# Joined row statistics for the two heads of a pair in the first batch of an attention and two-FFN kernel

## The chip, the cores and the metric

The kernel runs on one core of a Trainium2 chip. The time is the device time of one execution in microseconds (us), and lower is better. The engines are called as in the profile: PE (TensorE: matmuls and transposes; PEld are its weight loads), DVE (VectorE), ACT (ScalarE), POOL (GpSimd) and SP (SyncE, which issues most of the transfers). Each engine works through its own list in order and waits on semaphores of the others.

## The reference

Causal attention with a decay bias, then two feed-forward layers (FFNs), all in float32:

```python
def _attn_ref(q, k, v, s):          # 4 batches, 8 heads, 576 positions, 64 columns
    scores = q @ k.T / sqrt(D)
    cum = np.cumsum(np.maximum(s, 0.0), axis=-1)
    bias = -(cum[:, :, :, None] - cum[:, :, None, :])
    scores = np.where(causal, -1e9, scores + np.minimum(bias, 0.0))
    scores = scores - np.max(scores, axis=-1, keepdims=True)
    attn = np.exp(scores)
    attn = attn / (np.sum(attn, axis=-1, keepdims=True) + 1e-09)
    return attn @ v
# FFN 1: h = x @ w_in (512 -> 1024), softmax-gated, normalised, @ w_out (1024 -> 512), 2304 tokens
# FFN 2: h = x @ w2_in (512 -> 2048), h * clip(h + 3, 0, 6) / 6, @ w2_out (2048 -> 512)
```

The change lies in the attention: the maximum of each row of scores, and the reciprocal of each row's sum.

## The kernel before

The work is staged in three plans. The first holds all of the attention, the decoding of FFN 1's weights and most of FFN 1; the others hold the rest of FFN 1 and FFN 2. In a plan, each piece of work is added with its engine, a cost, and the names of what it reads and writes; `Plan.emit` then walks through time with these costs and writes out one list for each engine, always taking the earliest added piece that is ready. So the order on every engine follows from all the costs and dependencies together, and one piece more or less can move many others. Scores and FFN products share eight PSUM banks (`bank`), which the plan hands out too.

Attention goes by heads. A head's 576 rows are cut into five tiles t = 0 to 4 of 128, 128, 128, 96 and 96 rows; tile t needs the columns up to its own end, so tile 4 has 576 columns, too many for one bank, and comes in two pieces of 288. In batch 0 the two heads of a pair are worked on together (`qk_whole`, four pairs); later batches take one head at a time (`qk`). For each piece PE makes the scores (L545 in batch 0, L572 later), and `tops` on DVE (L501) adds the mask, copies the piece to SBUF (`y`) and puts the negated row maximum into `nmax`. For tile 4 the maxima of the two pieces are joined by `both` (L509). ACT then takes the exponential in place (L513) and puts the row sums into `sums`. When a head's five tiles are done, `norm` makes the reciprocals on DVE (L583, L584 into `rsum`), and POOL multiplies the five tiles by them (L588). PE transposes the blocks (L634), DVE and ACT copy them out (L638), PE multiplies them with V (L663), and DVE and ACT copy the result into `x` (L670). In batch 0's pairs 1 and 3 the score tiles lie in the buffers named zhy and zly. The last pair of batch 0 is normalised by `norm_part`, which already takes both heads in a call (L601, L602, L606).

Between these the plan puts the decoding of the weights, which come as 64-bit numbers: a load issued by ACT (raw_wi, L301), a step on ACT (L307), three on DVE (L311, L316, L319), one on POOL (L323), the high part (L329 or L331) and the low part on POOL (L337). Queries and keys are loaded by SP (rawq, rawk, L383), and values too (V, L395 and L396). From pair 4 on (batch 1) they are turned on PE (L451), split into high and low parts (HL4q and the like, L459 and L463; pair 4's keys use the free end of w_out_l), and copied by SP into two operand buffers stack0 and stack1, one for each head of a pair (L469, L470); the gate rows, rows_d, are loaded into them last (L473). The first L572 of a head needs all of these. FFN 1 follows: L740 for h, L751 to L781 for its statistics, L806 to L813 for the transposed parts zh and zl, and L827 for its output.

## Time and profile before

| what | value |
|---|---|
| median of 3 timed runs | 854.26 us (854.06 to 858.12) |
| span of the profiled execution | 851.3 us, so the median lies 2.96 us above it |
| PE, DVE, ACT, POOL busy | 813.4, 484.0, 399.2, 226.6 us |
| batch 0's pieces of L509, and of L583 with L584 before the joined pair 3 | 8, and 6 of each |

Busy time is that of the engine's own instructions. The span runs from the first to the last instruction; the timed runs have a small part around it. Batch 0 and the turn to batch 1 lie in the first 100 us or so.

### The profile page before, as it was taken

Reading aid. Unit: us, or ns where it says so; the run is one execution under the profiler, and the core shown is the slowest. Engines: PE = TensorE matmul, PEld = TensorE weight load, DVE = VectorE, ACT = ScalarE, POOL = GpSimd, SP = SyncE. Lnnn points to the kernel's source line nnn. Section 1 sums busy time; section 2 is a strip of 40 time slices with the busy share of each in tenths; the row PEclk is TensorE's granted clock in tenths of the full one; section 3 lists DMA queues with packets and bytes.
Section 4 is the critical chain, followed back from the end, with each engine's and each line's share of the span. In section 5 each row is a group of like instructions: output and inputs, shape, how many; then the busy total and the mean of one; then the engine's idle time right before and its main releaser. Section 6 shows DMA issues by size and latency. Waiting matters only on the chain.

```text
span 851.3 us, 13524 instructions
## 1 busy us (share of the span) xinstructions
PE 813.4 (96%) x4816; PEld 686.6 (81%) x4816; DVE 484.0 (57%) x1205; ACT 399.2 (47%) x928; POOL 226.6 (27%) x323
## 2 busy tenths in 40 slices
PE   3997899999999999999999999999999999999998
PEld 2565677888898889887798999998888888888886
DVE  4898999556755575648746999843222232222221
ACT  2776767646665465635444555444222322232222
POOL 1686666334533263325320112100000000000000
PEclk9999999999999999999999999999999999999999
DMA  6569476655555455233304444112000300010001
GB/s 167 129 156 204 124 172 135 151 125 114 128 137 126 98 115 125 63 111 108 104 32 162 143 129 137 63 62 87 0 1 2 99 0 1 1 49 1 1 1 50
DMA packets 93667, 76.85 MB, mean 90 GB/s; under 512 B 62080, under 2 KB 75904, under 8 KB 93600
## 3 DMA queue, kind: packets, MB, share of 16 engines
q1 hardware_dynamic: 91296, 67.60, 31.4%
q10 hardware_dynamic: 2304, 8.39, 3.1%
q8 instruction: 38, 0.62, 0.3%
q14 instruction: 29, 0.24, 0.1%
HBM read 44.71 MB, written 10.03 MB: 64 GB/s over the span
## 4 chain that ended last, share of the span: by engine, by line
PE 79%; DVE 11%; DMA 4%; POOL 3%; issue 1%; ACT 1%; SPq 0%; ACTq 0%; DVEq 0%; POOLq 0%
PE bank L986 23%; PE bank L1017 23%; PE bank L827 11%; PE bank L740 8%; PE bank L663 4%; PE bank L572 4%; PE bank L634 4%; PE bank L806 1%; DVE y L501 1%; PE bank L451 1%; POOL y L588 1%; DMA rawk<-in_k_dram 1%; DVE st L751 1%; DMA stack<-rows_d 1%; PE bank L545 1%
## 5 line engine op out<-in xcount | busy, mean ns | idle before, releaser
L986 PE MATMUL bank<-x2h,w 128*128 128x512 f32 (+1 forms) x640 | 185.4, 371 | 0.0
L1017 PE MATMUL bank<-w,gh 128*128 128x512 f32 x576 | 178.5, 393 | 0.6 <-ACT gh L998 0.6
L994 DVE SCALAR_TENSOR_TENSOR g<-g,bank 128x512 f32<-128x512 f32 (+1 forms) x80 | 50.5, 632 | 184.1 <-ACT g L990 183.9
L986 PEld LDWEIGHTS bank<-x2h,w 128*128 128x128 f32 x640 | 118.6, 188 | 18.7
L990 ACT ACTIVATE g<-bank 128x512 f32<-128x512 f32 (+1 forms) x80 | 44.4, 555 | 176.4 <-PE bank L986 176.1
L1017 PEld LDWEIGHTS bank<-w,gh 128*128 128x128 f32 x576 | 107.8, 188 | 23.2 <-ACT gh L998 1.2
L986 PE MATMUL bank<-x2l,w 128*128 128x512 f32 (+1 forms) x320 | 118.5, 370 | 0.0
L1017 PE MATMUL bank<-w,gl 128*128 128x512 f32 x288 | 111.4, 391 | 0.0
L588 POOL TENSOR_SCALAR y<-y,rsum 128x128 f32<-128x128 f32 (+4 forms) x140 | 80.7, 593 | 99.7 <-DVE rsum L584 55.4
L501 DVE CUSTOM_DVE_ANT_0 y<-bank,mask 96x288 f32<-96x288 f32 (+4 forms) x168 | 74.1, 466 | 48.0 <-PE bank L572 38.8
L513 ACT ACTIVATE y<-y,nmax 128x256 f32<-128x256 f32 (+4 forms) x140 | 83.5, 597 | 32.9 <-DVE nmax L501 26.8
L827 PE MATMUL bank<-zh,w_out_h 128*128 128x256 f32 x288 | 83.2, 289 | 0.3 <-DVE nmax L501 0.3
L827 PE MATMUL bank<-zl,w_out_h 128*128 128x256 f32 x288 | 81.2, 282 | 1.9 <-DVE zl L813 1.9
L827 PE MATMUL bank<-zh,w_out_l 128*128 128x256 f32 x288 | 81.0, 281 | 0.0
L1002 DVE TENSOR_TENSOR gl<-g,gh 128x512 fp32r<-128x512 f32 (+1 forms) x80 | 56.2, 703 | 36.2 <-ACT gh L998 35.5
L998 ACT CAST gh<-g 128x512 fp32r<-128x512 f32 (+1 forms) x80 | 46.1, 577 | 46.2 <-DVE g L994 45.7
L986 PEld LDWEIGHTS bank<-x2l,w 128*128 128x128 f32 x320 | 60.0, 188 | 8.2
L1017 PEld LDWEIGHTS bank<-w,gl 128*128 128x128 f32 x288 | 54.1, 188 | 11.9
L572 PE MATMUL bank<-stack 128*96 128x288 f32 (+4 forms) x288 | 58.9, 318 | 4.9 <-DMA stack<-rows_d 2.3
L740 PE MATMUL bank<-w_in_h,xh 128*128 128x512 f32 x144 | 61.5, 427 | 1.1 <-DVE xh L722 0.6
L740 PE MATMUL bank<-w_in_h,xl 128*128 128x512 f32 x144 | 58.0, 403 | 1.0 <-POOL xl L726 1.0
L740 PE MATMUL bank<-w_in_l,xh 128*128 128x512 f32 x144 | 57.7, 401 | 0.0
(170 smaller groups left out, 1388.6 us busy)
## 6 DMA issues: line engine op xcount, KB each, us to landing
raw_w2i<-in_moe_w_in_dram SPq DMA_DIRECT2D x16, 512.0 KB
raw_w2o<-in_moe_w_out_dram SPq DMA_DIRECT2D x16, 512.0 KB
rawq<-in_q_dram SPq DMA_DIRECT2D x32, 144.0 KB
rawk<-in_k_dram SPq DMA_DIRECT2D x32, 144.0 KB
x_d<-x2s SPq DMA_DIRECT2D x36, 128.0 KB
out_dram<-ob SPq DMA_DIRECT2D x18, 256.0 KB
raw_wi<-in_moe_w_in_dram ACTq DMA_DIRECT2D x8, 512.0 KB
raw_wo<-in_moe_w_out_dram ACTq DMA_DIRECT2D x8, 512.0 KB
```

Of the source, the lines that this page charges most:

```text
L501: nc.vector.tensor_tensor_reduce(out=ys[h, t][:n, c0:c1], in0=bank(key)[:n, : c1 - c0], in1=mask[:n, 480 + n - w + c0 : 480 + n - w + c1], ...
L513: nc.scalar.activation(out=y[:n], in_=y[:n], func=AF.Exp, bias=nmax[:n, h, t : t + 1], scale=-1.0, accum_out=sums[:n, h, t : t + 1])
L572: nc.tensor.matmul(bank(key)[:n, : c1 - c0], lhsT=ss[:, 2 - 2 * m, ST[t] : w], rhs=ss[:, 3 - 2 * m, c0:c1], start=(m == 0), stop=(m == 1))
L588: nc.gpsimd.tensor_scalar(ys[h, t][:n], ys[h, t][:n], rsum[:n, h, t : t + 1], 1.0, ALU.mult, ALU.mult)
L740: nc.tensor.matmul(bank(key), lhsT=xs[i][m // 2][:, kk, :], rhs=(w_in_l if m == 1 else w_in_h)[:, kk, f * 512 : (f + 1) * 512], start=(kk ...
L827: nc.tensor.matmul(bank(key)[:, : 2 * P], lhsT=w[:, kk, m * P : (m + 1) * P], rhs=z[:, kk, :], start=(kk == 0 and i == 0), stop=(kk == KFF ...
L986: nc.tensor.matmul(bank(key)[:, :w], lhsT=wt[:, a, 0, c * P : (c + 1) * P], rhs=x[:, c, :w], start=(c == 0 and i == 0), stop=(c == KDM - 1 ...
L990: nc.scalar.activation(out=g_t[ci, m][0][:, :w], in_=bank(key)[:, :w], func=AF.Relu, bias=3.0, scale=1.0)
L994: nc.vector.scalar_tensor_tensor(out=gg, in0=gg, scalar=6.0, in1=bank(key)[:, :w], op0=ALU.min, op1=ALU.mult)
L998: nc.scalar.copy(gh[:, :w], gg[:, :w])
L1002: nc.vector.tensor_sub(gl[:, :w], gg[:, :w], gh[:, :w].bitcast(F32))
L1017: nc.tensor.matmul(bank(key), lhsT=g_t[ci, m][1 + i // 2][:, t * P : (t + 1) * P], rhs=w2[m][:, i % 2, 1, :], start=(m == 0 and i == 0), s ...
```

## The change

For batch 0 the join of the two pieces' maxima, and the reciprocals of the row sums, are done in one call for both heads of a pair. In `pieces`, `norm` now gets the list of heads, which has one head in the later batches. The multiplications on POOL are added in the order tile by tile, head by head within a tile, where before one head's five came first. The line numbers shift: L509 becomes L510, L513 L514, L572 L573, L583 and L584 L586 and L587, L588 L591, L634 and L638 L638 and L642, L663 L667, L740 L744, L827 L831.

```diff
-    def exps(h, t, pieces):
+    def exps(heads, t, pieces):
         n, w = SZ[t], ST[t] + SZ[t]
+        hs = slice(heads[0], heads[-1] + 1)
 
         def both():
-            nc.vector.tensor_tensor(nmax[:n, h, t : t + 1], nmax[:n, h, t : t + 1], nmax[:n, h, NQ : NQ + 1], ALU.min)
-
-        def exp():
+            nc.vector.tensor_tensor(nmax[:n, hs, t : t + 1], nmax[:n, hs, t : t + 1], nmax[:n, hs, NQ : NQ + 1], ALU.min)
+
+        def exp(h):
             y = ys[h, t]
...
         if len(pieces) > 1:
-            plan.add("DVE", 0.2, both, reads=[f"nmax{h}_{NQ}"], writes=[f"nmax{h}_{t}"])
+            plan.add("DVE", 0.2, both, reads=[f"nmax{h}_{NQ}" for h in heads], writes=[f"nmax{h}_{t}" for h in heads])
...
-    def norm(h):
+    def norm(heads):
+        hs = slice(heads[0], heads[-1] + 1)
+
         def inv():
-            nc.vector.tensor_scalar_add(rsum[:, h, :], sums[:, h, :], 1.0e-9)
-            nc.vector.reciprocal(rsum[:, h, :], rsum[:, h, :])
+            nc.vector.tensor_scalar_add(rsum[:, hs, :], sums[:, hs, :], 1.0e-9)
+            nc.vector.reciprocal(rsum[:, hs, :], rsum[:, hs, :])
...
-        plan.add("DVE", 0.34, inv, reads=[f"sums{h}_{t}" for t in range(NQ)], writes=[f"rsum{h}"])
+        plan.add("DVE", 0.36, inv, reads=[f"sums{h}_{t}" for h in heads for t in range(NQ)], writes=[f"rsum{h}" for h in heads])
         for t in range(NQ):
-            plan.add("POOL", 0.27 + 0.00085 * (ST[t] + SZ[t]), lambda t=t: go(t), reads=[f"rsum{h}", f"{y_key(h, t)}/e"], writes=[f"{y_key(h, t)}/n"])
+            for h in heads:
+                plan.add("POOL", 0.27 + 0.00085 * (ST[t] + SZ[t]), lambda h=h, t=t: go(h, t), reads=[f"rsum{h}", f"{y_key(h, t)}/e"], writes=[f"{y_key(h, t)}/n"])
...
-            elif x == "n":
-                r.extend((0.0, lambda h=h: norm(h)) for h in last)
+            elif x == "n" and last:
+                r.append((0.0, lambda: norm(last)))
```

On DVE, the list at the reciprocals of pair 0 (e_wi and a_wi are the second block of w_in in decoding, HL the queries and keys of pair 2):

```order
 L501 ISA nmax 128x1
-L583 TENSOR_SCALAR rsum<-sums 128x5
-L584 RECIPROCAL rsum<-rsum 128x5
-L316 TENSOR_SCALAR e_wi_0_326<-a_wi_0_300 128x512
-L583 TENSOR_SCALAR rsum<-sums 128x5
-L584 RECIPROCAL rsum<-rsum 128x5
-L319 SCALAR_TENSOR_TENSOR e_wi_0_326<-raw_wi_0_159,e_wi_0_326 128x512
+L316 TENSOR_SCALAR e_wi_0_319<-a_wi_0_300 128x512
+L319 SCALAR_TENSOR_TENSOR e_wi_0_319<-raw_wi_0_159,e_wi_0_319 128x512
+L586 TENSOR_SCALAR rsum<-sums 128x10
+L587 RECIPROCAL rsum<-rsum 128x10
 L420 COPY HL_265<-bank_102 128x288
```

Four calls became two, and they moved behind the two decode steps. On POOL, the multiplications of pair 0 (y_0 to y_4 are tiles, a_wi and w_in_l as above); before:

```order
L337 TENSOR_TENSOR w_in_l<-a_wi_0_173,w_in_h 128x512
L588 TENSOR_SCALAR y_0_175<-y_0_175,rsum 128x128
L588 TENSOR_SCALAR y_1_191<-y_1_191,rsum 128x256
L588 TENSOR_SCALAR y_2_212<-y_2_212,rsum 128x384
L588 TENSOR_SCALAR y_3_224<-y_3_224,rsum 96x480
L588 TENSOR_SCALAR y_4_238<-y_4_238,rsum 96x576
L588 TENSOR_SCALAR y_0_176<-y_0_176,rsum 128x128
```

and now:

```order
L337 TENSOR_TENSOR w_in_l<-a_wi_0_173,w_in_h 128x512
L323 TENSOR_TENSOR a_wi_0_300<-a_wi_0_300,e_wi_0_319 128x512
L591 TENSOR_SCALAR y_0_175<-y_0_175,rsum 128x128
L591 TENSOR_SCALAR y_0_176<-y_0_176,rsum 128x128
L591 TENSOR_SCALAR y_1_191<-y_1_191,rsum 128x256
L591 TENSOR_SCALAR y_1_192<-y_1_192,rsum 128x256
L591 TENSOR_SCALAR y_2_212<-y_2_212,rsum 128x384
```

The heads alternate, and the decode step L323 moved ahead of all ten. On SP's queue, the loads at the turn to batch 1 (numbers behind the names are pairs, for stack the head of the pair); before:

```order
L383 DMA rawk5_664<-in_k_dram 96x6x64 x2
L395 DMA V3_631<-in_v_dram 128x3x64
L396 DMA V3_631<-in_v_dram 96x2x64
L469 DMA stack0_109<-w_out_l_85 64x576
L470 DMA stack0_109<-w_out_l_85 64x2x576
L469 DMA stack1_110<-HL4q_531 64x576
L470 DMA stack1_110<-HL4q_531 64x2x576
L473 DMA stack0_109<-rows_d_71 4x2x576
L383 DMA rawq6_762<-in_q_dram 96x6x64 x2
L469 DMA stack1_110<-w_out_l_85 64x576
L470 DMA stack1_110<-w_out_l_85 64x2x576
```

and now:

```order
L383 DMA rawk5_648<-in_k_dram 96x6x64 x2
L395 DMA V3_618<-in_v_dram 128x3x64
L396 DMA V3_618<-in_v_dram 96x2x64
L469 DMA stack1_110<-HL4q_575 64x576
L470 DMA stack1_110<-HL4q_575 64x2x576
L469 DMA stack0_109<-w_out_l_85 64x576
L470 DMA stack0_109<-w_out_l_85 64x2x576
L383 DMA rawq6_725<-in_q_dram 96x6x64 x2
L469 DMA stack1_110<-w_out_l_85 64x576
L470 DMA stack1_110<-w_out_l_85 64x2x576
L473 DMA stack0_109<-rows_d_71 4x2x576
L473 DMA stack1_110<-rows_d_71 4x2x576
```

Stack0's gate rows moved behind rawq6 and behind stack1's keys. On PE at the same place, the product with V of pair 2 (L663, in the changed kernel L667) stood after the first L572 for its last eight matmuls by number of rows, and is now done before the first L573, as are the first transposes of pair 3 (zhy3, zly3).

## Rows read from the trace of the kernel before

**Rows 1.** The page: span, and busy time of each engine.
```profile
span 851.3 us, 13524 instructions
PE 813.4 (96%) x4816; PEld 686.6 (81%) x4816; DVE 484.0 (57%) x1205; ACT 399.2 (47%) x928; POOL 226.6 (27%) x323
```

**Rows 2.** Busy time by stretches: length, engines (x instructions), granted clock, DMA, GB/s.
```profile
20.00:140.00 120.00, 106.32 (x733) 78.25 (x732) 107.08 (x322) 82.23 (x220) 82.26 (x102) 0.96 0.69 162
140.00:200.00 60.00, 58.68 (x461) 51.93 (x459) 37.76 (x130) 36.14 (x101) 22.71 (x38) 1.00 0.53 123
48.00:50.00 2.00, 1.00 (x9) 0.83 (x10) 2.00 (x7) 0.61 (x3) 2.00 (x3) 1.00 0.67 155
50.00:54.00 4.00, 4.00 (x27) 3.23 (x27) 2.96 (x12) 2.53 (x7) 2.66 (x3) 0.57 0.26 78
58.00:75.00 17.00, 13.93 (x102) 9.17 (x101) 12.81 (x43) 11.02 (x31) 12.32 (x18) 0.90 1.05 218
68.00:70.00 2.00, 0.14 (x1) 0.17 (x2) 1.41 (x4) 1.86 (x5) 1.19 (x3) 1.00 1.22 203
70.00:74.00 4.00, 4.00 (x22) 2.39 (x23) 1.20 (x5) 0.70 (x2) 3.02 (x6) 0.60 1.08 210
```

**Rows 3.** Instructions of L509, L583 and L584 from 20 to 205 us.
```profile
L509 DVE TENSOR_TENSOR nmax<-nmax x19: 145/214/1610, 26.8 to 201.1; 96x1 f32<-96x1 f32 x19
L583 DVE TENSOR_SCALAR rsum<-sums x16: 158/164/1219, 28.6 to 197.7; 128x5 f32<-128x5 f32 x16
L584 DVE RECIPROCAL rsum<-rsum x16: 189/189/192, 28.8 to 197.9; 128x5 f32<-128x5 f32 x16
```

**Rows 4.** DVE in order of time: start, length, instruction.
```profile
37.84 0.40 DVE L509 TENSOR_TENSOR nmax<-nmax 96x1 f32<-96x1 f32 x2
...
39.83 0.69 DVE L319 SCALAR_TENSOR_TENSOR e_wi<-raw_wi,e_wi 128x512 f32<-128x512 uint32 x1
40.44 0.16 DVE L583 TENSOR_SCALAR rsum<-sums 128x5 f32<-128x5 f32 x1
...
40.74 1.22 DVE L583 TENSOR_SCALAR rsum<-sums 128x5 f32<-128x5 f32 x1
...
67.79 1.03 DVE L509 TENSOR_TENSOR nmax<-nmax 96x1 f32<-96x1 f32 x1
```

**Rows 5.** POOL in order of time, pairs 0 and 1.
```profile
29.21 5.89 POOL L588 TENSOR_SCALAR y<-y,rsum 128x128 f32<-128x128 f32 x10 [2.09 <-DVE rsum L584]
...
40.67 1.26 POOL L323 TENSOR_TENSOR a_wi<-a_wi,e_wi 128x512 f32<-128x512 f32 x1 [2.51 <-DVE rsum L583]
41.91 0.82 POOL L588 TENSOR_SCALAR zhy<-zhy,rsum 128x128 f32<-128x128 f32 x2
```

**Rows 6.** DVE in order of time at the turn; in brackets the idle time before.
```profile
70.48 0.56 DVE L501 CUSTOM_DVE_ANT_0 y<-bank,mask 128x384 f32<-128x384 f32 x1 [1.04 <-PE bank L572]
...
74.05 0.29 DVE L501 CUSTOM_DVE_ANT_0 y<-bank,mask 128x128 f32<-128x128 f32 x1 [2.33 <-PE bank L572]
```

**Rows 7.** The chain of work that ended last: start, length, what.
```profile
65.49 4.24 DMA stack<-rows_d
...
70.44 2.94 PE bank L663 x16
```

**Rows 8.** DMA issues from 50 to 82 us: KB each.
```profile
stack<-w_out_l SPq DMA_DIRECT2D x2, 288.0 KB
...
stack<-w_out_l SPq DMA_DIRECT2D x2, 144.0 KB
rawq<-in_q_dram SPq DMA_DIRECT2D x2, 144.0 KB
```

**Rows 9.** DVE in order of time, pair 4's keys and what follows.
```profile
58.48 0.82 DVE L463 SCALAR_TENSOR_TENSOR w_out_l<-bank,w_out_l 128x288 fp32r<-128x288 f32 x2
59.22 0.55 DVE L501 CUSTOM_DVE_ANT_0 zhy<-bank,mask 128x384 f32<-128x384 f32 x1
...
61.30 0.64 DVE L501 CUSTOM_DVE_ANT_0 zhy<-bank,mask 96x480 f32<-96x480 f32 x1
```

More of the change, by code (lines that the diff above doesn't have):

```diff
@@ L515, in exps @@
         if len(pieces) > 1:
-            plan.add("DVE", 0.2, both, reads=[f"nmax{h}_{NQ}"], writes=[f"nmax{h}_{t}"])
-        plan.add("ACT", act(w, 0.46), exp, reads=[f"nmax{h}_{t}"] + [f"{y_key(h, t)}/{c0}" for c0, _, _ in pieces], writes=[f"{y_key(h, t)}/e", f"sums{h}_{t}"])
+            plan.add("DVE", 0.2, both, reads=[f"nmax{h}_{NQ}" for h in heads], writes=[f"nmax{h}_{t}" for h in heads])
+        for h in heads:
+            plan.add("ACT", act(w, 0.46), lambda h=h: exp(h), reads=[f"nmax{h}_{t}"] + [f"{y_key(h, t)}/{c0}" for c0, _, _ in pieces], writes=[f"{y_key(h, t)}/e", f"sums{h}_{t}"])
     def pieces_of(t):
@@ L559, in qk_whole @@
                          writes=[f"{y_key(h, t)}/{c0}", f"nmax{h}_{at}"])
-        for h in heads:
-            exps(h, t, pieces)
+        exps(heads, t, pieces)
     def qk(h, t):
@@ L578, in qk, with go @@
             plan.add("DVE", dve(c1 - c0), lambda c0=c0, c1=c1, at=at, key=key: tops(h, t, c0, c1, at, key), reads=[key], writes=[f"{y_key(h, t)}/{c0}", f"nmax{h}_{at}"])
-        exps(h, t, pieces)
-    def norm(h):
+        exps((h,), t, pieces)
+    def norm(heads):
+        hs = slice(heads[0], heads[-1] + 1)
         def inv():
-            nc.vector.tensor_scalar_add(rsum[:, h, :], sums[:, h, :], 1.0e-9)
-            nc.vector.reciprocal(rsum[:, h, :], rsum[:, h, :])
-        def go(t):
+            nc.vector.tensor_scalar_add(rsum[:, hs, :], sums[:, hs, :], 1.0e-9)
+            nc.vector.reciprocal(rsum[:, hs, :], rsum[:, hs, :])
+        def go(h, t):
             n = SZ[t]
             nc.gpsimd.tensor_scalar(ys[h, t][:n], ys[h, t][:n], rsum[:n, h, t : t + 1], 1.0, ALU.mult, ALU.mult)
-        plan.add("DVE", 0.34, inv, reads=[f"sums{h}_{t}" for t in range(NQ)], writes=[f"rsum{h}"])
+        plan.add("DVE", 0.36, inv, reads=[f"sums{h}_{t}" for h in heads for t in range(NQ)], writes=[f"rsum{h}" for h in heads])
         for t in range(NQ):
-            plan.add("POOL", 0.27 + 0.00085 * (ST[t] + SZ[t]), lambda t=t: go(t), reads=[f"rsum{h}", f"{y_key(h, t)}/e"], writes=[f"{y_key(h, t)}/n"])
+            for h in heads:
+                plan.add("POOL", 0.27 + 0.00085 * (ST[t] + SZ[t]), lambda h=h, t=t: go(h, t), reads=[f"rsum{h}", f"{y_key(h, t)}/e"], writes=[f"{y_key(h, t)}/n"])
     def norm_part(heads, part):
```

## The prediction

> **What bounds the kernel now.** I read the page's head first. TensorE (PE) is busy for 813.4 of 851.3 us [rows 1], so all that any edit can win back is the 37.9 us in which PE stands still, plus what it loses at the low clock. Then I cut the span into stretches, because the edit touches batch 0 alone. From 20 to 140 us PE is busy for 106.32 of 120 us and VectorE (DVE) for 107.08; from 140 to 200 us PE is busy for 58.68 of 60 and DVE for only 37.76 [rows 2]. The reader is to see two regimes: up to about 140 us DVE and PE share the limit, each 89% busy and each waiting for the other; after that PE alone sets the pace, and PE can only win what it got earlier from the first regime. So I look for what delays DVE before 140 us, and for what stops PE there.
>
> PE stops are dear. It stands still for 1.0 us from 48 to 50 and for 1.86 us from 68 to 70, and after each the granted clock is 0.57 or 0.60 for 4 us [rows 2], a mixture of the two levels, 1.2 and 2.4 GHz. At the high level those 4 us would have taken about 4 x 0.57 = 2.3, so a drop costs PE 1.7 us.
>
> **The sum: what is removed.** Joining takes ten instructions off DVE: four joins of maxima (L509; batch 0 has four pairs with two pieces at t = 4), three L583 and three L584 (pairs 0 to 2; pair 3 was joined before, while later batches take one head at a time). Nothing is added: a joined call handles 2 or 10 elements a partition in place of 1 or 5. Lower bound: the shortest of each, 4 x 0.145 + 3 x (0.158 + 0.189) = 1.62 us [rows 3]. Upper bound: the second call of each pair as it ran. Two L509 together took 0.40 us, so 0.20 each for three of them, and the fourth took 1.03; two L583 are put at the median of 0.164 and the one at 40.74 took 1.22; three L584 at 0.189. That is 0.60 + 1.03 + 0.33 + 1.22 + 0.57 = 3.75 us [rows 3, 4]. The joined call itself is a form that this trace does not show; it is nearest to the single one. I take the middle, **2.7 us off DVE**.
>
> The two long calls are a mechanism of their own. L583 at 40.44 took 0.16 us; the one at 40.74 took 1.22 and ended when GpSimd's (POOL's) L323, begun at 40.67 and 1.26 long, ended [rows 4, 5]. Such a call stands still behind a POOL instruction that got in first. The Trainium skill (SBUF — State Buffer, section Who interferes with whom) states this as an exclusive lock on a pair of ports that the two engines share: whichever of a DVE instruction of this kind and a POOL instruction comes second is blocked for the whole of the first. This speaks against the change as much as for it, since the order now puts the joined L586 of pairs 0 and 2 right behind L319, whose end lets POOL's L323 go. By the rule alone each could cost 1.27 us. I don't put that in the sum, for the row at 40.44 stands right behind L319 (39.83, 0.69 us) too and got in before POOL [rows 4, 5]; it is a rival below.
>
> **What moves.** The calls end one list and begin another: the planner orders every engine anew from the first joined call on, and only after the second FFN tile pair (the rows of zh1) do the orders agree again. Three places matter.
>
> *Pair 0 on POOL.* The joined call waits for the sums of both heads and stands behind L316 and L319, so POOL now runs the decode step L323 (1.26 us, the length of the one at 40.67) ahead of the ten multiplications (5.89 us), and these alternate between the heads [rows 5]. Head 0's tiles come later. What hides it: the order gives DVE all of pair 1's L501 and the copies of pair 3 before the first transposed block is wanted. Bounds 0 (hidden) and 1.26 (not); I take **+0.6 us**.
>
> *Pair 1 on POOL.* The joined call now precedes L311 to L319 of the next decode on DVE and L323 on POOL, where before the first multiplication waited for all of them until 41.91 [rows 5]. The transposes that PE lacked when it stood still from 48 to 50 hang on these. I count nothing for it, as DVE was busy for all of those 2 us [rows 2].
>
> *The turn to batch 1.* Here DVE waited 1.04 us before 70.48 and 2.33 us before 74.05, both for PE's L572 [rows 6]: first stack0's gate rows landed only at 65.49 + 4.24 = 69.73 [rows 7], then PE ran 16 attention matmuls in 2.94 us before the next L572 [rows 7]. In the new order those matmuls, and the first transposes of pair 3, stand ahead of the first L573, so the 2.33 us should go. But on the queue the gate rows are issued behind rawq6 and stack1's two key loads, 2 x 144 + 288 + 144 = 720 KB [rows 8]; at the 218 GB/s that the DMA engines moved from 58 to 75 us (share 1.05, full) [rows 2] these are 0.737 MB / 218 GB/s = 3.4 us. With DVE's lead of 2.7 us the rows land between 67.0 and 70.4. DVE, ready before at 70.48 - 1.04 = 69.44, is ready at 66.7 and has some 0.8 us more in front of the waiting instruction (half of the two L463 at 0.82, and one pair like L583 and L584 [rows 3, 9]): 67.5. From landing to L501 took 0.75 us (69.73 to 70.48). So it waits between 0.3 and 3.7 us where it waited 3.37; middle 2.0, **-1.4 us**.
>
> Sum on DVE: -2.7 + 0.6 - 1.4 = -3.5 us. Of this I let through the share for which DVE is busy in the stretch, 0.89: -3.1 us. The profiled span of 851.3 us becomes 848.2; the median of the timed runs, 854.26, lies 3.0 above that span, and I leave that gap as it is. **Predicted: 851.2 us.** Its own range comes from the bounds: best (-3.75 - 3.1) x 0.89 = -6.1, worst (-1.62 + 1.26 + 0.3) = -0.1, so 848.2 to 854.2.
>
> **The rivals.**
>
> *More than that (848 us).* Both PE stops, at 48 and at 68 us, vanish because their work now comes earlier, and with them two low-clock stretches of 1.7 us each: 851.2 - 3.4 = 847.8. For it: pair 1's multiplications start earlier, and the turn gives PE attention matmuls to do while it waits. Against it: PE is not the only bound there, and a PE that runs faster waits longer.
>
> *Nothing arrives (854 us).* The joined calls of pairs 0 and 2 are blocked behind L323 as the call at 40.74 was, 2 x (1.22 - 0.16) = 2.1 us [rows 4], which leaves 2.7 - 2.1 = 0.6 of the lead, and POOL's +0.6 eats it. This is the rule of the skill cited above. For it the call at 40.74, against it the one at 40.44.
>
> *Slower (857 us): the gate rows come late.* In the new order the second L463 of pair 4's keys is parted from the first by four L501, two of 0.55 and two of 0.64 us, 2.4 us in all; before, the two ran back to back in 0.82 us [rows 9]. Stack0's keys wait for it, the queue is in order, and the 3.4 us of other loads come on top: the gate rows land at 69.73 + 2.4 + 3.4 = 75.5, DVE goes on at 76.3, 8.8 us after it is ready in place of 3.4. That is +5.4 - 2.7 = +2.7 us, 857.0, with POOL's term or one more clock drop beyond 858.5. It decides from the landing on: after 67.5 + 3.37 + 2.7 - 0.75 = 72.8 us the change loses time. For it: full DMA engines; against it: V2 no longer stands ahead of rawq4 on the queue, so loads start sooner.
>
> **How the numbers follow.** Forecast 0.42, more 0.20, nothing 0.18, late gate rows 0.20. Half a per cent, 4.3 us, is about what a measurement of this kernel tells from no change: faster means below 850.0. Most of "more" (0.17) and the lower third of the forecast's range (0.13) lie there: 0.30. Above 858.5 lies somewhat under half of "late gate rows", 0.08, and 0.02 for what I didn't think of: 0.10. The rest is 0.60. The range runs from 847 to 857: it takes in "more" and the point of the late rows and leaves out the tails on both sides.
>
> **What would show it.** Right: DVE has ten instructions fewer; L586 stays near 0.16 us; stack0's gate rows land before 71; DVE waits less than 3.4 us in all at the first L573; the first FFN matmul and the first L831 come 2 to 4 us earlier, and from about 180 us on every row is earlier by the same amount. Wrong: an L586 above 1 us; gate rows that land after 72.8; a PE stop of over 1 us and a clock below 0.7 at a place where there was none; or a lead at 80 us that is gone at 140, which would mean that DVE's list after the turn, and not what stands before it, sets the time.

## The result and the profile after

The changed kernel takes 858.69 us (median of 6 runs, 856.70 to 861.85), the kernel before 854.16 beside it: ratio 1.0054, 95% interval 1.0032 to 1.0076, so 4.6 us slower (2.7 to 6.5). That lies above the range that was forecast.

The profiled execution of the changed kernel took 861.03 us, 2.3 us above the median, and at 0.980 it has the lowest mean clock of the six (the others 0.984 to 0.992). So its trace shows more of the loss than a usual run has: 7.9 us of span, where the mean span of the six runs is 4.2 us longer than the mean before (the table of all runs below). Its page answers to [rows 1]:

```profile
span 859.2 us, 13503 instructions
PE 821.3 (96%) x4816; PEld 693.6 (81%) x4816; DVE 485.9 (57%) x1195; ACT 399.9 (47%) x928; POOL 225.5 (26%) x323
```

The ten instructions are gone (1205 to 1195), but DVE is busy for 1.9 us more, and PE does the same 4816 matmuls in 7.9 us more. The busy times by stretches, as in [rows 2], and three stretches more (columns: length, PE, PEld, DVE, ACT, POOL busy, granted clock, DMA share, GB/s):

```profile
20.00:140.00 120.00, 107.44 (x679) 78.65 (x680) 106.51 (x306) 80.27 (x213) 80.47 (x101) 0.89 0.62 154
140.00:200.00 60.00, 60.00 (x493) 53.52 (x492) 37.46 (x122) 35.52 (x97) 21.83 (x36) 1.00 0.56 129
50.00:54.00 4.00, 4.00 (x36) 2.70 (x38) 3.91 (x13) 2.80 (x8) 1.42 (x2) 1.00 0.17 60
58.00:75.00 17.00, 14.85 (x102) 9.95 (x99) 14.81 (x42) 12.28 (x34) 15.82 (x23) 0.90 1.01 216
33.00:41.00 8.00, 7.78 (x50) 6.83 (x50) 5.94 (x22) 4.73 (x12) 5.00 (x8) 0.57 0.53 140
101.00:112.00 11.00, 8.87 (x36) 7.12 (x37) 10.79 (x33) 9.03 (x23) 9.42 (x12) 0.54 0.82 209
129.00:136.00 7.00, 5.36 (x16) 4.42 (x17) 6.33 (x20) 4.23 (x10) 4.18 (x6) 0.51 0.53 133
```

The last three in the trace of before:

```profile
33.00:41.00 8.00, 7.85 (x74) 5.33 (x72) 7.01 (x24) 5.92 (x17) 4.95 (x7) 1.00 0.30 89
101.00:112.00 11.00, 8.10 (x40) 6.45 (x41) 9.86 (x33) 7.86 (x20) 8.79 (x12) 0.84 1.08 224
129.00:136.00 7.00, 6.27 (x44) 5.29 (x42) 6.84 (x22) 5.54 (x15) 5.73 (x7) 1.00 1.08 218
```

From 20 to 140 us PE is busy for 1.1 us more than before, and still issues 679 matmuls where it issued 733. The column that differs is the clock: 0.89 against 0.96. The three stretches at the end run near 0.5, the lower of the two levels (1.2 GHz). In the trace of before the same three stand at 1.00, 0.84 and 1.00. Work lost to the clock is busy time times what lacks to 1: 7.78 x 0.43 + 8.87 x 0.46 + 5.36 x 0.49 = 10.0 us, against 8.10 x 0.16 = 1.3 before. The drop at 50 us [rows 2] is gone, worth 4 x 0.43 = 1.7. That makes 10.0 - 1.3 - 1.7 = 7.0 us of work. These are not 7.0 of the 7.9 us by which this span grew: PE also stood still for 2.4 us less from 20 to 200 us, and the delay can be read from one and the same work in both traces (PE in order of time, in each pair before and then now):

```profile
197.44 0.69 PE L572 MATMUL bank<-stack 128*128 128x384 f32 x4
201.12 0.69 PE L573 MATMUL bank<-stack 128*128 128x384 f32 x4
```

```profile
529.99 0.62 PE L1017 MATMUL bank<-w,gh 128*128 128x512 f32 x2
537.88 0.62 PE L1021 MATMUL bank<-w,gh 128*128 128x512 f32 x2
```

From some 185 us on the lists of all engines agree again, and PE is 3.7 us behind. The other 4.2 us of this span come later, most of them between 358 and 530 us, in lists that are the same. So the part of the span that changed holds about half of the difference of the two profiled executions, and nearly as much as the 4.2 us of the means.

Now the joined calls. First a group view of the joins of maxima and of the reciprocals from 20 to 75 us (shortest, median and longest in ns), answering to [rows 3], then DVE in order of time:

```profile
L510 DVE TENSOR_TENSOR nmax<-nmax x4: 213/993/1232, 26.9 to 66.2; 96x2 f32<-96x2 f32 x4
L586 DVE TENSOR_SCALAR rsum<-sums x3: 161/166/167, 29.6 to 58.2; 128x10 f32<-128x10 f32 x3
L587 DVE RECIPROCAL rsum<-rsum x3: 216/216/217, 29.8 to 58.4; 128x10 f32<-128x10 f32 x3
```

```profile
34.76 1.23 DVE L510 TENSOR_TENSOR nmax<-nmax 96x2 f32<-96x2 f32 x1
54.18 0.96 DVE L510 TENSOR_TENSOR nmax<-nmax 96x2 f32<-96x2 f32 x1
66.21 1.02 DVE L510 TENSOR_TENSOR nmax<-nmax 96x2 f32<-96x2 f32 x1
67.49 0.92 DVE L605 TENSOR_SCALAR rsum<-sums 128x4 f32<-128x4 f32 x1
70.43 1.25 DVE L605 TENSOR_SCALAR rsum<-sums 128x6 f32<-128x6 f32 x1
```

L586 stayed at 0.16 to 0.17. But the four joined L510 took 0.21 + 1.23 + 0.96 + 1.02 = 3.42 us, where the eight single L509 of batch 0 took 2.25. The reciprocals took 3.23 us in twelve calls (six L583 with 2.09, six L584 with 1.14) and now 0.50 + 0.65 = 1.15 in six. So from trace to trace DVE won 3.23 - 1.15 - (3.42 - 2.25) = 0.9 us at these places, where 2.7 was forecast. And L605, which the change does not touch, took 0.92 and 1.25 where it (then L601) took 0.15 and 0.16 before.

Last, five starts on PE: the transposes of pair 3's queries, those of pair 2's blocks, the first scores of batch 1, the first FFN tile's transposes, and the third FFN tile (PE in order of time; in brackets the idle time before), and POOL at pair 0, answering to [rows 5]:

```profile
32.92 0.69 PE L413 MATMUL bank<-ident,rawq 96*128 96x96 f32 x6 [1.33 <-DMA rawq<-in_q_dram]
66.47 2.99 PE L638 MATMUL bank<-ident,y 96*128 96x96 f32 x22 [1.58 <-POOL y L591]
73.34 0.77 PE L573 MATMUL bank<-stack 128*128 128x384 f32 x4
103.19 1.97 PE L810 MATMUL bank<-ident,e 128*128 128x128 f32 x8 [1.33 <-POOL e L785]
130.64 0.80 PE L744 MATMUL bank<-w_in_h,xh 128*128 128x512 f32 x1 [2.15 <-DVE st L765]
```

```profile
29.82 1.27 POOL L323 TENSOR_TENSOR a_wi<-a_wi,e_wi 128x512 f32<-128x512 f32 x1 [2.72 <-DVE rsum L586]
31.07 5.63 POOL L591 TENSOR_SCALAR y<-y,rsum 128x128 f32<-128x128 f32 x10
```

POOL's first multiplication of pair 0 starts at 31.07 in place of 29.21. PE has a stop of 1.33 us ahead of the low clock at 33, one of 1.33 us up to 103.19 and one of 2.15 us up to 130.64; in these two the clock falls. The first and the last are not there before. At the second place PE stops before too, for 1.46 us up to 102.07, but the clock stays at 1.00 until some 108 us.

### The profile page after: what moved, and what is told of

It is laid out like the page before. It is cut to its first block, busy times and chain, and to the rows that moved or that the text cites. A ratio compares the mean times of both kernels' runs of the same rounds, so it can differ in the third digit from the quotient of the medians.

```text
span 859.2 us, 13503 instructions
## 1 busy us (share of the span) xinstructions
PE 821.3 (96%) x4816; PEld 693.6 (81%) x4816; DVE 485.9 (57%) x1195; ACT 399.9 (47%) x928; POOL 225.5 (26%) x323
## 4 chain that ended last, share of the span: by engine, by line
PE 85%; DVE 8%; DMA 3%; POOL 2%; ACT 1%; issue 1%; DVEq 0%; POOLq 0%; SPq 0%; ACTq 0%
PE bank L990 23%; PE bank L1021 22%; PE bank L831 12%; PE bank L744 10%; PE bank L667 5%; PE bank L638 5%; PE bank L573 4%; PE bank L810 2%; PE bank L451 1%; DVE y L501 1%; PE bank L547 1%; POOL y L591 1%; DMA stack<-HL12k 1%; DVE st L755 1%; DMA xr<-x_d 1%
## 5 line engine op out<-in xcount | busy, mean ns | idle before, releaser
L591 POOL TENSOR_SCALAR y<-y,rsum 128x256 f32<-128x256 f32 (+4 forms) x140 | 81.4, 599 | 98.7 <-DVE rsum L587 54.4
L514 ACT ACTIVATE y<-y,nmax 128x256 f32<-128x256 f32 (+4 forms) x140 | 83.3, 596 | 35.3 <-DVE nmax L501 29.2
L831 PE MATMUL bank<-zh,w_out_h 128*128 128x256 f32 x288 | 83.8, 291 | 0.0
L831 PE MATMUL bank<-zl,w_out_h 128*128 128x256 f32 x288 | 81.9, 284 | 1.9 <-DVE zl L817 1.9
L831 PE MATMUL bank<-zh,w_out_l 128*128 128x256 f32 x288 | 81.8, 284 | 0.0
L744 PE MATMUL bank<-w_in_h,xh 128*128 128x512 f32 x144 | 62.1, 431 | 4.1 <-DVE st L765 2.2
L573 PE MATMUL bank<-stack 128*96 128x288 f32 (+4 forms) x288 | 60.5, 324 | 5.3 <-DMA stack<-HL12k 1.7
L744 PE MATMUL bank<-w_in_h,xl 128*128 128x512 f32 x144 | 58.5, 406 | 0.4 <-POOL xl L730 0.4
L744 PE MATMUL bank<-w_in_l,xh 128*128 128x512 f32 x144 | 58.2, 404 | 0.0
```

The lines of the kernel that those rows point to most:

```text
L514: nc.scalar.activation(out=y[:n], in_=y[:n], func=AF.Exp, bias=nmax[:n, h, t : t + 1], scale=-1.0, accum_out=sums[:n, h, t : t + 1])
L573: nc.tensor.matmul(bank(key)[:n, : c1 - c0], lhsT=ss[:, 2 - 2 * m, ST[t] : w], rhs=ss[:, 3 - 2 * m, c0:c1], start=(m == 0), stop=(m == 1))
L591: nc.gpsimd.tensor_scalar(ys[h, t][:n], ys[h, t][:n], rsum[:n, h, t : t + 1], 1.0, ALU.mult, ALU.mult)
L744: nc.tensor.matmul(bank(key), lhsT=xs[i][m // 2][:, kk, :], rhs=(w_in_l if m == 1 else w_in_h)[:, kk, f * 512 : (f + 1) * 512], start=(kk ...
L831: nc.tensor.matmul(bank(key)[:, : 2 * P], lhsT=w[:, kk, m * P : (m + 1) * P], rhs=z[:, kk, :], start=(kk == 0 and i == 0), stop=(kk == KFF ...
```

## The experiments

All on one core, each timed in five rounds beside the kernel before (the two stop kernels in one). Differences in us are the ratio's against 854.4.

### Calls or order?

*calls_only.* The planner works as before; its lists are then kept, and each joined call is issued where the second head's call stood. The first head's call is left out, and what hangs on it follows behind the joined one. Every engine's list is that of before, less ten DVE instructions.

```diff
         for _, i in sorted(order):
+            if i in self.pair:
+                first.add(i)
+                continue
+            if self.ops[i][3] & (first | set(held)):
+                held.append(i)
+                continue
             self.ops[i][2]()
...
-            nc.vector.tensor_tensor(nmax[:n, h, t : t + 1], nmax[:n, h, t : t + 1], nmax[:n, h, NQ : NQ + 1], ALU.min)
+            nc.vector.tensor_tensor(nmax[:n, hs, t : t + 1], nmax[:n, hs, t : t + 1], nmax[:n, hs, NQ : NQ + 1], ALU.min)
```

> Every engine keeps the order of the kernel before; only the ten joined-away VectorE instructions are gone, each joined call standing where the second of its pair stood. Theory 'order' (the time is set by the list that the planner gives, the ten instructions are worth a little): 851.5 to 854.2 us, ratio 0.997 to 1.000; no low-clock stretch at 33 to 41 us. Rival 'calls' (a call that waits for both heads, or is slow itself, is what costs): 857 to 860 us, ratio 1.004 to 1.007, with the first L591-like multiplication of pair 0 late and a clock drop behind it.

858.61 us, ratio 1.0048 (1.0033 to 1.0064): +4.1.

*plan_only.* The reverse: the lists of the changed kernel, but each entry issues the single calls.

```diff
         def both():
-            nc.vector.tensor_tensor(nmax[:n, hs, t : t + 1], nmax[:n, hs, t : t + 1], nmax[:n, hs, NQ : NQ + 1], ALU.min)
+            for h in heads:
+                nc.vector.tensor_tensor(nmax[:n, h, t : t + 1], nmax[:n, h, t : t + 1], nmax[:n, h, NQ : NQ + 1], ALU.min)
...
-            nc.vector.reciprocal(rsum[:, hs, :], rsum[:, hs, :])
+            for h in heads:
+                nc.vector.tensor_scalar_add(rsum[:, h, :], sums[:, h, :], 1.0e-9)
+                nc.vector.reciprocal(rsum[:, h, :], rsum[:, h, :])
```

> The planner's entries and with them every engine's order are those of the changed kernel, but each entry issues the single calls of the kernel before, so no instruction is saved. Theory 'order': 858.5 to 861.5 us, ratio 1.005 to 1.0085, with the clock drop at 33 to 41 us and the long ones at 101 to 112 and 129 to 135. Rival 'calls' (joined calls themselves are slow): 853 to 856 us.

863.26 us, ratio 1.0107 (1.0091 to 1.0124): +9.1. The same instructions as before in another order cost 9.1 us. In that order the joined calls are worth something: 863.26 to 858.69, 4.6 us by the medians. DVE in the trace of plan_only, where L511 and L588 are the single calls:

```profile
30.14 1.22 DVE L588 TENSOR_SCALAR rsum<-sums 128x5 f32<-128x5 f32 x1
36.44 1.83 DVE L511 TENSOR_TENSOR nmax<-nmax 96x1 f32<-96x1 f32 x2
55.41 1.14 DVE L511 TENSOR_TENSOR nmax<-nmax 96x1 f32<-96x1 f32 x2
59.84 1.21 DVE L588 TENSOR_SCALAR rsum<-sums 128x5 f32<-128x5 f32 x1
68.87 1.64 DVE L511 TENSOR_TENSOR nmax<-nmax 96x1 f32<-96x1 f32 x2
```

The single calls are long at the same places, so it is the place and not the joined form that makes L510 long. In this order the maxima took 4.99 us in eight calls and the reciprocals 4.18 in twelve, against 3.42 and 1.15 joined: 4.6 us of DVE's time. (The two profiled spans lie only 1.5 us apart, 860.7 and 859.2.) In the order of before the joins won 2.3 us of DVE's time: in calls_only the two kinds took 2.03 and 1.17, against 2.25 and 3.23. Yet in the order of before the joined calls cost 4.1 us. So neither theory holds as stated: the order costs most, and what ten calls fewer do depends on the order.

*max_only, norm_only.* One half of the change each, planned anew. The diff is the last part of max_only's against the changed kernel; norm_only has the other half undone, exps.

```diff
-            elif x == "n" and last:
-                r.append((0.0, lambda: norm(last)))
+            elif x == "n":
+                r.extend((0.0, lambda h=h: norm(h)) for h in last)
```

> Only the joins of the maxima are made for both heads; the reciprocals stay one head at a time. Theory 'order': the list is new from the first join on, so the time may lie anywhere from 851 to 860 us and need not add up with its counterpart. Rival 'waiting for both heads' sums costs nothing here (the joins of maxima are short): 853 to 854.5 us, ratio 0.999 to 1.000.

> Only the reciprocals are made for both heads, and GpSimd's multiplications go tile by tile; maxima joined one head at a time. Theory 'order': anywhere from 851 to 860 us. Rival 'the joined reciprocal alternates the heads on GpSimd and lets L323 go first, so the first transposes come late': all of the loss is here, 857.5 to 859.5 us, ratio 1.004 to 1.006, with a PE stop at 30 to 36 us and a clock drop at 33 to 41.

max_only 858.87 (1.0050, 1.0037 to 1.0063), norm_only 855.74 (1.0014, 0.9996 to 1.0032). Four joins of maxima, the smaller half, bring +4.3 us when the planner reorders; the rival that puts the loss on the reciprocals falls.

### Which call, with the order held

*calls_max, calls_norm.* As calls_only, with one kind of call joined; the diff is of calls_max against calls_only, less the lines of inv, and calls_norm has the same for the maxima.

```diff
-        join("inv", h, plan.add("DVE", 0.34, inv, reads=[f"sums{h}_{t}" for t in range(NQ)], writes=[f"rsum{h}"]))
+        (plan.add("DVE", 0.34, inv, reads=[f"sums{h}_{t}" for t in range(NQ)], writes=[f"rsum{h}"]))
```

> Order of the kernel before; only the four second joins of maxima are gone. Theory 'both heads' (a reciprocal joined for both heads keeps the first head's multiplications of pair 0 back by 0.8 us, and that is what costs): 853.3 to 854.5 us, ratio 0.9985 to 1.000. Rival 'any shift' (the kernel before is at a lucky spot, and any small shift of work in batch 0 brings more PE stops with a low clock behind them): 856 to 859 us, ratio 1.002 to 1.005.

> Order of the kernel before; only the reciprocals of pairs 0 to 2 are joined, each at the place of the second head's. Theory 'both heads': the whole loss of the joined calls in this order is here, 857.5 to 859.5 us, ratio 1.0035 to 1.0055. Rival 'any shift': 855 to 859, not told apart by this run alone.

calls_max 855.03 (0.9997, 0.9985 to 1.0010), calls_norm 858.01 (1.0032, 1.0016 to 1.0048). With the order held the joins of maxima cost nothing, so the 4.3 us of max_only are the new order's.

*late_single, pool_late.* Does it cost that head 0 of pair 0 waits for head 1? First the two heads' single calls side by side at the second's place (late_single), then POOL's tiles behind the first one some 0.8 us later and all else as before (pool_late; the factors -0.5, in halfs, and -2 leave the values as they are).

```diff
+            for g in range(h // 2 * 2, h // 2 * 2 + 2) if h < H else (h,):
+                nc.vector.tensor_scalar_add(rsum[:, g, :], sums[:, g, :], 1.0e-9)
+                nc.vector.reciprocal(rsum[:, g, :], rsum[:, g, :])
```

```diff
             nc.gpsimd.tensor_scalar(ys[h, t][:n], ys[h, t][:n], rsum[:n, h, t : t + 1], 1.0, ALU.mult, ALU.mult)
+            for _ in range(2 if h == 0 and t == 0 else 0):
+                nc.gpsimd.tensor_scalar(ys[h, t][:n], ys[h, t][:n], halfs[:n], -2.0, ALU.mult, ALU.mult)
```

> Order of the kernel before, no instruction less: the first head's reciprocals of pairs 0 and 2 are only moved behind to stand beside the second head's. Theory 'both heads': the wait without any saving, 858 to 861 us, ratio 1.004 to 1.0075, at least as slow as with joined reciprocals. Rival 'the form of the joined call' (10 elements, 2 in place of 5 and 1): 853.5 to 855 us.

> The kernel before with two more GpSimd instructions of about 0.4 us each behind the first multiplication of pair 0 (times -0.5 and times -2, so that values stay): GpSimd hands out pair 0's tiles 0.8 us later and nothing else changes. Theory 'both heads' (late first tiles cost): 857 to 859 us, ratio 1.003 to 1.005. Rival 'the wait of DVE costs, not GpSimd': 853.5 to 855 us.

late_single 855.40 (1.0005, 0.9988 to 1.0021), pool_late 856.12 (1.0010, 0.9993 to 1.0027). In the traces POOL's first multiplication of pair 0 starts at 30.22 in late_single, 1.0 us after that of before, and in pool_late the two added ones take 1.34 us. Waiting for both heads costs less than can be measured here, at most 1.8 and 2.3 us by the intervals. The theory that it is the whole loss falls.

*norm_p1, norm_p02, all_but_p1.* calls_norm for pair 1 alone and for pairs 0 and 2 alone; then calls_only without pair 1's reciprocals. The diff is of norm_p1 against calls_norm; norm_p02 has (0, 2) there.

```diff
-        if h < H and h % 2:
+        if h < H and h % 2 and h // 2 in (1,):
             plan.twins.append((single[what, h - 1], op))
```

> Order of the kernel before, the reciprocals joined for pair 1 alone (two VectorE calls fewer, both of which stood side by side already, so no call waits for more than before). Theory 'given back beside GpSimd' (the 1.0 us won there is lost in L311 and L316, which then run beside GpSimd's multiplications): DVE is 1 us earlier at 44 us and not earlier at 50; 854 to 858 us, ratio 0.9995 to 1.004. Rival 'waiting for both heads' sums': a gain, 852.5 to 854 us, ratio 0.997 to 0.9995.

> Order of the kernel before, the reciprocals joined for pairs 0 and 2 alone. Theory 'given back beside GpSimd': as late_single, 854 to 855.5 us, ratio 0.9995 to 1.001. Rival 'waiting for both heads' sums': the loss of calls_norm is here, 856.5 to 858.5 us, ratio 1.002 to 1.005.

> Order of the kernel before, eight VectorE calls fewer: all the joins of calls_only but pair 1's reciprocals. Theory 'pair 1' (its call turns the rest into a loss): 852.5 to 854 us, ratio 0.998 to 0.9997, faster than either kernel. Rival 'any join shifts the list against GpSimd, the loads and TensorE' (no single call is to blame): 855.5 to 859 us, ratio 1.001 to 1.005.

norm_p1 854.39 (0.9992, 0.9975 to 1.0008), norm_p02 854.11 (0.9993, 0.9981 to 1.0005), all_but_p1 855.04 (1.0002, 0.9984 to 1.0020). None of the parts costs or gains anything that can be told, though two of them together (calls_norm) cost 2.7, and all_but_p1 with pair 1's call added (calls_only) 4.1. Only norm_p1's inner story can be read. DVE in the two traces; in these kernels L331, L336 and L339 are the decode steps L311, L316 and L319, L440 is L420, L611 is L583, and L666 is L638. With pair 1 joined (norm_p1):

```profile
40.95 0.17 DVE L611 TENSOR_SCALAR rsum<-sums 128x10 f32<-128x10 f32 x1
43.17 0.82 DVE L440 COPY HL<-bank 128x288 f32<-128x288 f32 x2
45.52 1.80 DVE L331 TENSOR_SCALAR a_wi<-a_wi 128x512 int32<-128x512 int32 x1
47.36 0.58 DVE L336 TENSOR_SCALAR e_wi<-a_wi 128x512 int32<-128x512 int32 x1
48.85 0.61 DVE L666 COPY pt<-bank 128x448 f32<-128x448 f32 x1
```

With pair 1 single (norm_p02):

```profile
40.99 0.17 DVE L611 TENSOR_SCALAR rsum<-sums 128x5 f32<-128x5 f32 x1
41.29 1.23 DVE L611 TENSOR_SCALAR rsum<-sums 128x5 f32<-128x5 f32 x1
44.07 0.81 DVE L440 COPY HL<-bank 128x288 f32<-128x288 f32 x2
46.33 0.42 DVE L331 TENSOR_SCALAR a_wi<-a_wi 128x512 int32<-128x512 int32 x1
46.78 1.22 DVE L336 TENSOR_SCALAR e_wi<-a_wi 128x512 int32<-128x512 int32 x1
48.80 0.61 DVE L666 COPY pt<-bank 128x448 f32<-128x448 f32 x1
```

The second L611 with its 1.23 us goes, and the copies at 43.17 come 0.90 us earlier. Then L331 takes 1.80 us in place of 0.42, beside POOL's multiplications (L336 then takes 0.58 in place of 1.22), and at 48.85 nothing is left. In this trace the saving was taken back by DVE's next instructions beside POOL.

### The clock

*before_fill, after_fill.* TensorE is kept busy while it waits, with transposes of the identity into a bank that the waiting instruction overwrites. The diff is of before_fill; after_fill has three such places.

```diff
             ss = stack_t[h % 2]
+            for _ in range(20 if (h, t, c0) == (8, 2, 0) else 0):
+                nc.tensor.transpose(bank(key)[:, :128], ident, ident)
```

> The kernel before with 20 transposes of the identity put ahead of the stack0 matmul that waits 2.28 us for the gate rows at 69.86 us; they go to the bank which that matmul overwrites, so TensorE is busy while it waits. Theory 'clock' (a PE stop brings a stretch at the low clock, and that stretch is what costs): the granted clock stays at 1.00 at 70 to 74 us, the mean clock of the run rises by 0.002, and the time falls by up to the 1.7 us of one drop: 853 to 854.3 us, ratio 0.998 to 0.9995. Rival 'symptom' (DVE and the loads set the pace there, the clock costs nothing): 854.5 to 856 us, ratio 1.000 to 1.0015.

> The changed kernel with TensorE kept busy at three of its data waits: 12 transposes of the identity ahead of pair 3's first query transposes (stop of 1.33 us before 32.92), 12 inside the transposes of head 4 that wait for GpSimd (1.58 us before 66.47), 10 ahead of the first FFN tile's transposes (1.33 us before 103.19), all in banks that are overwritten. Theory 'clock': the low stretches at 32 to 42 and 66 to 72 go and the one at 101 to 112 gets shorter, 3 to 6 us back: 853 to 856 us, ratio to before 0.998 to 1.002. Rival 'symptom': 858 to 861 us, ratio 1.004 to 1.008, the dummies costing what they take.

before_fill 854.95 (0.9991, 0.9972 to 1.0010), after_fill 857.74 (1.0027, 1.0007 to 1.0048). The first shows, in one trace, where such a gain went. Its stretches 70 to 74 (0.60 before [rows 2]) and 78 to 84, and the PE instruction between them:

```profile
70.00:74.00 4.00, 4.00 (x37) 3.09 (x36) 2.65 (x9) 1.38 (x4) 3.34 (x7) 1.00 1.09 225
78.00:84.00 6.00, 5.74 (x29) 5.76 (x30) 3.30 (x9) 2.31 (x6) 3.31 (x4) 0.50 0.82 219
```

```profile
78.26 2.31 PE L574 MATMUL bank<-stack 128*128 128x384 f32 x8 [2.61 <-DMA V<-in_v_dram]
```

The drop at 70 us is gone and PE does 37 matmuls there instead of 22. It then waits 2.61 us for loads where it waited 1.12, and the low clock comes at 78 instead. after_fill is 0.95 us below the changed kernel's median, not apart from it by the intervals. In its trace the clock stays at 1.00 from 33 to 41 and from 66 to 70 us, and falls in a stop of 2.85 us for the gate rows that ends at 72.91.

*stop_short, stop_long.* Seven PE stops where PE is otherwise never idle, in the second FFN: after a block of matmuls one DVE instruction (three in stop_long) reads its bank and rewrites the next operand with the same values.

```diff
+            if ci == 3 and m % 2 and m > 1 and c == KDM - 1:
+                gh = g_t[ci, m - 2][1][:, :w]
+                for _ in range(1):
+                    nc.vector.scalar_tensor_tensor(out=gh, in0=bank(key)[:, :w], scalar=0.0, in1=gh.bitcast(F32), op0=ALU.mult, op1=ALU.add)
```

> The kernel before with seven PE stops of about 1.2 us where TensorE never stood still (second FFN, chunk 3): after every second block of 12 matmuls one VectorE instruction reads its bank and rewrites the next operand with the same values. Theory 'clock, whatever the length': each stop costs its 1.2 us and 1.7 more, 874 to 876 us. Theory 'clock, long stops alone' (1.12 and 1.46 us stops before showed no drop, 1.56 did): 862 to 865 us at a clock as before. Rival 'a stop costs its length': the same 862 to 865.

> The same with three such VectorE instructions, stops of about 2.6 us. Theory 'clock': 7 x (2.6 + 1.7) = 30 us more, 883 to 886 us, with a low clock behind each stop. Rival 'a stop costs its length': 7 x 2.6 = 18 us more, 871 to 874 us, clock as before.

stop_short 861.02 (1.0074, 1.0048 to 1.0100), stop_long 874.78 (1.0227, 1.0184 to 1.0270). PE's waits from 680 to 780 us (total, times, longest), first of stop_short, then of stop_long with two of its stretches:

```profile
PE bank L1021 <- DVE gh L991: 5.5, 7, 0.8
```

```profile
PE bank L1021 <- DVE gh L991: 15.6, 7, 2.2
```

```profile
742.00:746.00 4.00, 3.60 (x16) 2.96 (x17) 1.73 (x3) 1.22 (x2) 0.00 (x0) 1.00 0.00 0
769.00:772.00 3.00, 2.67 (x6) 2.15 (x7) 1.54 (x3) 1.21 (x2) 0.00 (x0) 0.52 0.00 0
```

(gh L991 is the added instruction.) Stops of 0.78 us cost their length: 5.5 us by the trace, +6.3 (4.1 to 8.5) by the runs. Of the seven stops of 2.23 us the first six have the clock at 1.00 behind them (the fifth ends at 742.40), the last 0.52. So the theory that each long stop brings a drop falls; 15.6 us of stops and one drop of 1.7 make 17.3, within +19.4 (15.7 to 23.1; stop_long has two runs only).

### Places in the new order

*after_q3.* PE's transposes of pair 3's queries, which wait for their load until 32.92, go behind pair 0's first transposes; all else as in the changed kernel.

```diff
+            if self.until is not None and (i in self.hold or self.ops[i][3] & set(held)):
+                held.append(i)
+                continue
             self.ops[i][2]()
+            if i == self.until:
+                self.until = None
+                for j in held:
+                    self.ops[j][2]()
```

> The changed kernel, every engine in its order but for one place: TensorE's two groups of transposes of pair 3's queries, which stand ahead of pair 0's first transposes and wait for their load until 32.92 us, are put behind these. Theory 'planner's early load' (that stop and the low clock at 32 to 42 us are the first part of the loss): no stop over 1 us at 30 to 36, 854.5 to 857 us, ratio 1.000 to 1.0025. Rival 'the loss comes later anyway' (lists at the turn and in the first FFN): 857.5 to 859.5 us, ratio 1.0035 to 1.006.

858.45 us (1.0043, 1.0028 to 1.0058). The stop only changed its name; PE in order of time:

```profile
32.82 1.03 PE L648 MATMUL bank<-ident,y 128*128 128x128 f32 x6 [1.20 <-DVE nmax L511]
```

*jitter.* The kernel before, with the cost that the planner counts for one head's reciprocals changed as in the diff. The orders are those of before up to some 107 us, and no instruction comes or goes.

```diff
-        plan.add("DVE", 0.34, inv, reads=[f"sums{h}_{t}" for t in range(NQ)], writes=[f"rsum{h}"])
+        plan.add("DVE", 0.36, inv, reads=[f"sums{h}_{t}" for t in range(NQ)], writes=[f"rsum{h}"])
```

> The kernel before, same instructions, but the planner counts 0.36 in place of 0.34 us for a head's two reciprocal calls, as the changed kernel does for its joined ones; a few places of the orders change. Theory 'order' (any new order moves the time by several us, in either direction, without any work more or less): 851 to 860 us, at least 1.5 us off 854.4 more likely than not. Rival 'order is worth little': 853.5 to 855.3 us, ratio 0.999 to 1.001.

856.45 us (1.0027, 1.0014 to 1.0041): +2.3 us from 0.02 us in a planner's table. The trace shows at the third FFN tile the stop that the changed kernel has at 130.64, and the low clock behind it:

```profile
128.46 0.80 PE L740 MATMUL bank<-w_in_h,xh 128*128 128x512 f32 x1 [1.88 <-DVE st L761]
```

```profile
129.00:135.00 6.00, 6.00 (x20) 4.78 (x19) 5.90 (x19) 4.79 (x12) 4.85 (x8) 0.53 0.83 174
```

*after_34.* The changed kernel with 0.34 again for one head and 0.36 for two.

```diff
-        plan.add("DVE", 0.36, inv, reads=[f"sums{h}_{t}" for h in heads for t in range(NQ)], writes=[f"rsum{h}" for h in heads])
+        plan.add("DVE", (0.36 if len(heads) > 1 else 0.34), inv, reads=[f"sums{h}_{t}" for h in heads for t in range(NQ)], writes=[f"rsum{h}" for h in heads])
```

> The changed kernel, the planner charging 0.34 us for one head's reciprocals as before and 0.36 for two heads' joined ones; orders are those of the changed kernel up to some 115 us. Theory 'late order' (the 2.3 us of jitter are a part of the loss): no PE stop of 2.15 us and no low clock at 128 to 136 us, 855 to 857.2 us, ratio 1.001 to 1.003. Rival 'early order' (what is lost before 115 us is the loss): 857.5 to 860 us, ratio 1.004 to 1.006.

857.97 us (1.0038, 1.0022 to 1.0055). This order has a stop of 1.60 us before 133.38 in place of the 2.15 at 130.64, and the clock near 0.5 from 134 to 140 all the same. Whether the late part of the order is a share of the loss is not settled.

### All runs together

Each run lists its span and mean granted clock; (1 - clock) x span is the time by which the clock fell short. Means over each kernel's runs, those with added work left out:

| kernel | runs | span | short by clock | rest |
|---|---|---|---|---|
| before | 133 | 853.0 | 7.7 | 845.3 |
| norm_p1, norm_p02 | 12, 12 | 852.4, 852.5 | 8.1, 6.0 | 844.3, 846.5 |
| calls_max, all_but_p1 | 12, 12 | 853.0, 853.1 | 7.5, 6.3 | 845.5, 846.9 |
| late_single, norm_only | 12, 12 | 854.0, 854.0 | 8.4, 9.0 | 845.6, 844.9 |
| jitter, calls_norm | 12, 12 | 855.0, 855.5 | 9.5, 10.6 | 845.5, 845.0 |
| calls_only, after | 6, 6 | 856.2, 857.2 | 10.6, 11.1 | 845.7, 846.1 |
| after_34, after_q3, max_only | 12, 8, 5 | 856.3, 856.8, 856.9 | 12.7, 13.5, 12.7 | 843.6, 843.3, 844.3 |
| plan_only | 5 | 861.8 | 17.6 | 844.2 |

The spans differ by 9.4 us (852.4 to 861.8), the rest by 3.6, and in no order that follows the spans. What goes with the spans is how long PE runs at the low level. That this is what makes them longer is not shown: it is a sum over runs, and of the two fills, which did change the clock, before_fill brought the time short from 7.7 to 6.3 and after_fill from 11.1 to 7.0, but the rest rose to 846.4 and 848.5 with the dummies and the waits behind them. So of the 4.1 us less at the low clock in after_fill 1.7 us came out of the span.

## Why the prediction was wrong

**What failed.** The prediction let 0.89 of whatever DVE wins pass to the end, and let the orders matter at three places of which it costed two. plan_only refutes the second by itself: +9.1 us with every instruction kept. calls_only and norm_p1 refute the first: with every other engine's list kept, time won on DVE did not arrive (2.3 us won in calls_only, and the run 4.1 us slower).

**The term of the removed calls** (-2.7, bounds -1.62 to -3.75) fits the order of before, where calls_only won 2.3 us, but not the change as made, which also moved the calls: from the trace before to the one after the sites won 0.9 us, below the lower bound, while against single calls in the same new order (plan_only) the joins won 4.6, above the upper one. The joined L510 took 1.23, 0.96 and 1.02 us in place of pairs at 0.40, 0.28 and 1.18. The Trainium skill (SBUF — State Buffer, section Who interferes with whom) says that a DVE instruction with two SBUF inputs contends with a GpSimd instruction that reads SBUF; L510 is of that kind, and these three ran within stretches in which POOL was working (POOL's L591 from 31.07 to 36.70 in the first). The prediction applied that rule to L586 alone, which stayed at 0.16 to 0.17, so its rival "nothing arrives" was right in kind and wrong in place: L510, L605 and, in norm_p1, L331.

**Pair 0 on POOL** (+0.6, bounds 0 to 1.26) came out at 31.07 - 29.21 = 1.86 us later: POOL took L323 with its 1.27 us first, and that could start only at 29.82, behind DVE's L316 and L319, which now stand ahead of the joined call. By pool_late, with 1.34 us, such lateness costs 0.9 (-0.6 to 2.3), which the term's size can't be told from. *Pair 1 on POOL* was counted as nothing; the stop at 48 us and the drop behind it are gone, 1.7 us of the rival "more than that". Pair 2 on POOL was not among the three places: its first multiplication starts at 59.66 in place of 55.66, and PE stops for it until 66.47. In late_single, where it starts at 58.87, the run costs 0.4 us (-1.0 to 1.8), so that this lateness costs time at the end is not shown.

**The turn** (-1.4) went in its direction, by 0.5: DVE waited 2.9 us for L573 from 20 to 138 us, 1.84 the longest, against 3.4 before. But nothing there came earlier. The first L573 ran at 73.34, where the first L572 had run at 69.86, and the lead was gone before that: the first L463 of pair 4's queries started at 55.40 us in place of 54.34. In this trace PE had no wait for the gate rows. after_34, whose lists are the same up to some 120 us, has one:

```profile
76.28 0.79 PE L573 MATMUL bank<-stack 128*128 128x384 f32 x4 [2.13 <-DMA stack<-rows_d]
```

plan_only and after_q3 wait for them too, until 77.03 and 76.45. So the rival of late gate rows, which had them land at 75.5, is borne out in kind by these three; what it costs no run tells.

**The clock** was in the prediction as 1.7 us a drop, and used in one rival, as a gain of two drops. Its price fits the drop that went, but the three stretches that came lost 3.4, 4.1 and 2.6 us, and its share was wrong: the stretches lost 7.0 us more than before, while PE was 3.7 us behind at 201 us, and the mean over all runs has 3.4 us more at the low clock in a span 4.2 us longer. How much of the delay the low clock made, and how much the stops themselves, is not shown. Of the signs of being wrong one came true: a stop of over 1 us with a clock below 0.7 where there was none (32.92 and 130.64). A lead at 80 us that is gone at 140 did not, for there was no lead at 80: the first FFN matmul came at 83.60 in place of 82.02. At 140 the delay was larger, the first L831 at 140.6 against 130.8 for L827, though with 717 matmuls ahead of it where 705 had stood. How much order alone can do there jitter shows, with +2.3 us.

**Open.** Why calls_norm and calls_only cost 2.7 and 4.1 us while their parts cost nothing is not settled; the profiled execution of calls_only (854.88 us) was the shortest of its six and doesn't hold the loss. Nor does one trace of each tell: norm_p02 and calls_norm have the same lists up to pair 1's reciprocals, but reach these at 40.99 and 42.05 us. Nor is it settled what makes a stop bring a drop. No variant was faster than the kernel before by more than its interval.

## What to carry to other kernels

Where an order comes from a planner, an edit has two prices, that of the instructions and that of the new order. Time them apart: keep the lists and drop the calls, then keep the calls and take the new lists. Here the second was +9 us, and 0.02 us in a cost table was +2.3.

Before counting saved time on an engine that is 89% busy, look at its next instructions that share something with a neighbour; 0.9 us saved at 43 us was gone in the steps from 45.5. And sum the busy time lost to a low clock by stretch, in both traces, but check the sum: see how far behind one and the same instruction stands where the lists agree again, and by the spans and clocks of the other runs whether the profiled one is a usual one. Here it was not.

## What had not been expected of the hardware

A joined call with twice the elements was hardly longer by itself (L586 0.17 us at 10 elements a partition, L583 0.16 at 5), but L510 took up to 1.23 us beside POOL, and two single calls at that place 1.83. PE stops of 2.23 us in a stretch where PE is otherwise always busy left the clock at 1.00 six times of seven, while in batch 0, where PE also waits in between, drops stood behind stops of 1.33 us (changed kernel, 32.92) and 1.56 us (before, 49.00). Behind one of 1.46 us in batch 1 (before, 102.07) there was none, behind one of 1.33 at the same place (changed kernel, 103.19) there was. Keeping PE busy through one wait moved the drop to the next one, 8 us later.
